# Loading Q and K in 1-KB runs and restoring the token order after the transpose

## The chip, the cores and the metric

One core of a Trainium2 chip. The time is device microseconds of one execution. Runs of one kernel in the same rounds differ by up to 2.4%; comparisons use runs taken on the same chip in the same rounds. The engines: PE (TensorE), PEld (its weight loads), DVE (VectorE), ACT (ScalarE), POOL (GpSimd), SP (SyncE, which issues most DMAs).

## The reference, cut to what matters

```python
# q, k, v: 8 batches x 8 heads x 576 tokens x 64; w_in 512x2048; w_out 2048x512
scores = scale * q @ k.T ; mask: key in (query-64, query] ; attn = softmax(scores)
x = attn @ v                      # 4608 tokens x 512
h = x @ w_in ; g = h * clip(h + 3, 0, 6) / 6 ; out = g @ w_out
```

## The kernel before: the parts that matter

The tokens go through the feed-forward part in nine blocks of 512. Block T has a first phase (x @ w_in, eight chunks of 8 matmuls; for each chunk ScalarE makes t, VectorE makes gT) and a second (gT @ w_out, 64 matmuls). The attention of batch T+1 is slipped in between the second phase's matmuls as side units: S (scores of one pair of heads), PV, and so on. A small planner fixes, before anything runs, the order of instructions on every engine; at run time each engine takes its own list in order: in the prediction's views VectorE stands 3.05 us at a cast whose data have not landed, with a gT behind it.

Batches 2 to 7 load Q and K with one token to a partition, and a DMA transpose turns them:

```python
def load_nat(b):                                 # before; cut
    for i, src in enumerate((q, k)):
        for kb in range(KB):                     # 128 tokens at a time, 256-B runs
            nc.sync.dma_start(out=st.rearrange("p (h d) -> p h d", h=H),
                in_=src[b, :, kb*P : kb*P+ss, :].rearrange("h s d -> s h d"))
            ...                                  # GpSimd casts st into natural[i]
        ...                                      # then, on SP:
        nc.sync.dma_start_transpose(out=QK_tiles[...], in_=natural[i])
```

The scores of one pair of heads: 18 matmuls with the keys as weights and 64 queries as moving side, then exp on ScalarE in two parts, from PSUM into pT, then the mask on VectorE:

```python
for part in range(2):                            # before; cut
    st = two_banks(...)                          # one of 3 PSUM slots, shared with the first phase
    for i in range(i0, i1):
        for h in range(2):
            nc.tensor.matmul(st[:, h, c:c+D], lhsT=kwin(b, g, i, h),
                             rhs=QT[h*D:(h+1)*D, i*D:(i+1)*D], start=True, stop=True)
    nc.scalar.activation(out=pT[:, :, i0*D:i1*D], in_=st[:, :, 0:(i1-i0)*D], func=EXP, scale=scale)
```

V of these batches is loaded by DMAs that ScalarE issues between its own instructions.

The softmax here doesn't subtract the row's maximum and nothing guards it: scores larger than these inputs give would overflow.

## Time and profile before

| | |
|---|---|
| time, median of the 3 runs known at first | 313.49 us (310.9 to 315.31) |
| the profiled run | 315.82 us, span 314.1, mean granted clock 0.989 |
| busy share | PE 95%, DVE 51%, ACT 50%, POOL 38% |
| DMA packets under 512 B | 142,064 of 153,487 |

### The profile page before, as it was taken

What the parts mean: (1) busy time and instruction counts of PE and PEld (TensorE: products, weight loads), DVE (VectorE), ACT (ScalarE), POOL (GpSimd) and SP (SyncE); (2) the same over time, 40 slices, a digit from 0 to 9 for tenths busy, and PEclk for the clock granted to TensorE, in tenths of its full rate; (3) what the DMA queues carried; (4) which work ended last, traced back from release to release, by engine and by line L of the source; (5) the groups of instructions that cost most, each with busy time, mean ns of one, the idle gap of its engine ahead of it and who ended that gap; (6) DMA issues with size and microseconds to landing.
All of it is one profiled execution on the core that took longest, in us unless ns stands there. A gap on an engine that the chain in (4) does not pass through costs nothing.

```text
span 314.1 us, 6662 instructions
## 1 busy us (share of the span) xinstructions
PE 297.4 (95%) x2746; PEld 154.8 (49%) x2787; DVE 161.5 (51%) x206; ACT 157.7 (50%) x200; POOL 118.6 (38%) x186
## 2 busy tenths in 40 slices
PE   7989699889899999999999999999999999999996
PEld 3554345544444444685444444444575444444443
DVE  5576553855761666166616671667066607404610
ACT  5946556445723672367236723672367326315611
POOL 2257466614862484256325742384243000000000
PEclk9999969999999999999999999999999999999999
DMA  8999999999999999999999999999990530020011
GB/s 230 252 369 389 388 272 240 241 194 199 204 193 205 214 212 177 192 272 201 205 155 267 208 174 197 246 204 173 206 239 21 116 106 0 18 84 34 0 66 69
DMA packets 153487, 58.38 MB, mean 186 GB/s; under 512 B 142064, under 2 KB 143344, under 8 KB 153456
## 3 DMA queue, kind: packets, MB, share of 16 engines
q1 hardware_dynamic: 125184, 50.80, 77.2%
q10 hardware_dynamic: 28272, 7.15, 12.5%
q8 instruction: 22, 0.36, 0.5%
q14 instruction: 9, 0.07, 0.1%
HBM read 36.70 MB, written 9.44 MB: 147 GB/s over the span
## 4 chain that ended last, share of the span: by engine, by line
PE 78%; DMA 11%; DVE 3%; SPq 3%; POOL 2%; issue 2%; ACT 0%; POOLq 0%; ACTq 0%
PE acc L815 37%; PE ps L767 32%; DMA st<-in_k_dram 5%; PE ps L672 3%; DMA st<-in_v_dram 3%; DMA st<-in_moe_w_in_dram 3%; PE ps L648 3%; SPq L329 2%; POOL runs L277 1%; SPq L412 1%; DVE pT L614 1%; PE ps L562 1%; DVE opg L713 1%; DVE pT L618 1%; DVE QKT L274 0%
## 5 line engine op out<-in xcount | busy, mean ns | idle before, releaser
L779 DVE SCALAR_TENSOR_TENSOR gT<-t,ps 128x1024 bf16<-128x1024 bf16 x72 | 87.6, 1220 | 101.3 <-ACT t L776 101.2
L815 PE MATMUL acc<-wout,gT 128*128 128x512 bf16 (+2 forms) x560 | 130.3, 377 | 3.2 <-issue 2.6
L767 PE MATMUL ps<-xT,win 128*128 128x512 bf16 (+4 forms) x695 | 125.6, 340 | 0.5
L776 ACT ACTIVATE t<-ps,half 128x1024 bf16<-128x1024 f32 x72 | 79.8, 1113 | 50.6 <-PE ps L767 49.6
L767 PEld LDWEIGHTS <-win 128*128 128x128 bf16 x704 | 65.2, 98 | 59.3
L815 PEld LDWEIGHTS <-gT 128*128 128x128 bf16 x592 | 54.2, 99 | 59.9 <-issue 2.6
L832 ACT COPY osb<-acc 128x512 f32<-128x512 f32 (+2 forms) x37 | 21.3, 575 | 77.6 <-PE acc L815 74.0
L277 POOL CAST runs<-st 64x512 bf16<-64x512 f32 x48 | 30.0, 624 | 72.7 <-DMA st<-in_v_dram 67.9
L277 POOL CAST nat<-st 128x512 bf16<-128x512 f32 x48 | 34.3, 726 | 17.3 <-DMA st<-in_k_dram 11.7
L654 ACT ACTIVATE pT<-ps 128x640 bf16<-128x640 f32 (+1 forms) x48 | 28.8, 650 | 10.5 <-PE ps L648 10.5
L713 DVE TENSOR_TENSOR opg<-ps,rec 128x640 bf16<-128x640 f32 x32 | 26.4, 824 | 1.1
L658 DVE TENSOR_TENSOR pT<-pT,mask 128x1152 bf16<-128x1152 bf16 x24 | 20.0, 832 | 6.2 <-ACT pT L654 6.2
L277 POOL CAST V<-st 128x512 bf16<-128x512 f32 (+1 forms) x30 | 18.1, 604 | 5.0 <-DMA st<-in_v_dram 3.5
L602 ACT ACTIVATE pT<-ps 128x768 bf16<-128x768 f32 x16 | 12.6, 820 | 2.1 <-PE ps L593 2.1
L648 PEld LDWEIGHTS <-QKT 64*128 64x128 bf16 x432 | 7.7, 95 | 11.1 <-issue 11.1
L672 PE MATMUL ps<-runs,pT 128*64 128x65 bf16 x288 | 12.4, 197 | 0.2 <-POOL runs L277 0.2
L672 PEld LDWEIGHTS <-pT 128*64 128x64 bf16 x480 | 9.6, 111 | 6.0 <-issue 3.3
L710 DVE RECIPROCAL rec<-ps 128x10 f32<-128x10 f32 x32 | 7.0, 217 | 10.1 <-PE ps L672 8.6
L648 PE MATMUL ps<-QKT 64*128 64x64 bf16 x432 | 10.6, 191 | 1.3 <-DVE gT L779 0.8
L277 POOL CAST wout<-st 128x1024 bf16<-128x1024 f32 x8 | 9.1, 1167 | 6.5 <-DMA st<-in_moe_w_out_dram 6.5
L672 PE MATMUL ps<-V,pT 128*64 128x65 bf16 x192 | 11.5, 198 | 0.0
L562 PE MATMUL ps<-ident,runs 64*64 64x64 bf16 x288 | 7.0, 199 | 4.1 <-DVE gT L779 2.7
(60 smaller groups left out, 122.0 us busy)
## 6 DMA issues: line engine op xcount, KB each, us to landing
out_dram<-osb SPq DMA_DIRECT2D x35, 256.0 KB, 3.7
st<-in_q_dram SPq DMA_DIRECT2D x24, 256.0 KB, 6.4
st<-in_k_dram SPq DMA_DIRECT2D x24, 256.0 KB, 5.6
st<-in_v_dram ACTq DMA_DIRECT2D x24, 256.0 KB, 6.1
st<-in_moe_w_out_dram SPq DMA_DIRECT2D x4, 1024.0 KB, 13.6
st<-in_moe_w_in_dram SPq DMA_DIRECT2D x3, 1024.0 KB, 10.4
st<-in_q_dram SPq DMA_DIRECT2D x8, 288.0 KB, 6.8
st<-in_k_dram SPq DMA_DIRECT2D x8, 288.0 KB, 6.9
```

The costliest lines, as they stand in the source:

```text
L277: return lambda s: nc.gpsimd.tensor_copy(out=out_ap, in_=in_ap) and None
L602: nc.scalar.activation(out=pT[:, :, kbs[0] : kbs[0] + 2, 0:QW], in_=st[:, :, 0 : 2 * QW].rearrange("p h (k w) -> p h k w", k=2), func=EXP, ...
L648: nc.tensor.matmul(st[:, h, c : c + D], lhsT=kwin(b, g, i, h), rhs=QT[h * D : (h + 1) * D, i * D : (i + 1) * D], start=True, stop=True,)
L654: nc.scalar.activation(out=pT[:, :, i0 * D : i1 * D], in_=st[:, :, 0 : (i1 - i0) * D], func=EXP, scale=scale,)
L658: pl.op("DVE", t, 0.8, lambda s: nc.vector.tensor_tensor(out=pT.rearrange("p h (i w) -> p (h i) w", w=D), in0=pT.rearrange("p h (i w) -> p ...
L672: nc.tensor.matmul(o[odd * D : (odd + 1) * D, h, m * VW : (m + 1) * VW], lhsT=pT[:, h, i * D : (i + 1) * D], rhs=(V if i % 2 else W)[:, g, ...
L713: nc.vector.tensor_tensor(out=opg[:].rearrange("p k h d -> p h k d"), in0=ov[:, :, :, 0:D], in1=rec[:].unsqueeze(3).to_broadcast([P, 2, KB ...
L767: nc.tensor.matmul(hT[:, j, dst : dst + w], lhsT=win16[:, g, (2 * c + j) * P : (2 * c + j + 1) * P], rhs=xT[:, g, src : src + w], start=(g ...
L776: nc.scalar.activation(out=t1[:], in_=hT[:], func=RELU, bias=half[:], scale=1.0 / 6.0)
L779: nc.vector.scalar_tensor_tensor(out=gT[:, 2 * c : 2 * c + 2, :], in0=cell["t"][:], scalar=1.0, in1=hT[:], op0=MIN, op1=MULT,)
L815: nc.tensor.matmul(accs[ts][:, c0:c1], lhsT=gT[:, fc, ts * P : (ts + 1) * P], rhs=wout16[:, fc, c0:c1], start=(fc == 0), stop=(fc == NFC - 1),
L832: nc.scalar.copy(out=osb[:, c0:c1], in_=acc[:, c0:c1])
```

## The change

Its intent: four successive tokens to a partition make runs of 1 KB in place of 256 B, a quarter of the packets. The transpose then delivers the tokens in the order (j p) in place of (p j). Keys must be in token order for the windows, so five copies straighten K^T. Queries stay turned through the matmul, and exp's write puts them right.

```diff
+            for hh in range(2):                  # load: 4 tokens to a partition, 4 heads at a time
+                nc.sync.dma_start(out=T["t"][:, 4*hh : 4*hh+4, :],
+                    in_=src[b, 4*hh : 4*hh+4, 0 : J*P, :].rearrange("h (p j) d -> p h (j d)", j=J))
...
+            def straighten(t):                   # after K's transpose; POOL or DVE, as the planner finds
+                copy_op("kn", KN_ENG, NG*D, t, KN[:, :, D+J*P : D+S], Kp[:, :, J*P : S], None, one)
+                for g in range(NG):
+                    copy_op("kn", KN_ENG, J*P, t, KN[:, g, D : D+J*P].rearrange("d (p j) -> d p j", j=J),
+                            Kp[:, g, 0 : J*P].rearrange("d (j p) -> d p j", j=J), None, one)
...
-   nc.tensor.matmul(st[:, h, c:c+D], ..., rhs=QT[h*D:(h+1)*D, i*D:(i+1)*D])
+   nc.tensor.matmul(st[:, h, ...].rearrange("k (j i p) -> k i j p", ...)[:, i-i0], ..., rhs=turned(i)[...])
...
-   out=pT[:, :, i0*D:i1*D], in_=st[:, :, 0:(i1-i0)*D]
+   out=pT[:, :, i0*D:i1*D].rearrange("k h (p j) -> k h j p", j=J),
+   in_=st[:, :, 0:(i1-i0)*D].rearrange("k h (j p) -> k h j p", j=J)
...
-VGAP2 = 1.3                                      # pace of batch 2's V loads
+VGAP2 = 2.2
-FIRST = [(0, f, g) ...]                          # places of batch 1's side units
+FIRST = ((6, "T", 0), (12, "T", 1), (16, "S", 0), (0, "T", 2), ...)
```

More of the change, by code (lines that the diff above doesn't have):

```diff
@@ L23 @@
 NPT = 4
+KN_ENG = ("POOL", "DVE")
 VGAP = 1.8
-VGAP2 = 1.3
+VGAP2 = 2.2
 VRATE = 150
@@ L122 @@
     KB = (S + P - 1) // P
+    J = S // P
     SP = KB * P
@@ L197 @@
     W_ring = [runs_flat[:, i * NV : (i + 1) * NV].rearrange("p (g k h w) -> p g k h w", g=NG, k=KB, h=2) for i in range(2)]
+    KN = runs_flat[:, 2 * NV : 2 * NV + NG * (D + S)].rearrange("p (g t) -> p g t", g=NG)
     BL = S // D
@@ L246 @@
     pl.op("DVE", 26.2, 0.1, lambda s: nc.vector.tensor_copy(out=mask64[:], in_=m64[:]) and None, "mask64", deps=("m64",))
+    pl.op("DVE", 0.0, 0.2, lambda s: nc.vector.memset(KN[:, :, 0:D], 0.0) and None, "knz", deps=(("T", NR6 - 1, NG - 1),))
     for i, t in enumerate(W_ring):
@@ L281 @@
         "spread": lambda e, n: {"DVE": 0.156, "ACT": 0.165}[e] + {"DVE": 1.04e-3, "ACT": 0.83e-3}[e] * n,
+        "kn": lambda e, n: {"DVE": 0.08, "POOL": 0.18}[e] + {"DVE": 1.04e-3, "POOL": 0.83e-3}[e] * n,
         "x": lambda e, n: {"DVE": 0.156, "ACT": 0.165}[e] + {"DVE": 0.52e-3, "ACT": 0.83e-3}[e] * n,
@@ L426, in load_nat @@
             n = natural[i]
-            deps = stage_slot([("cast", b, i, j) for j in range(KB - 1)])
+            deps = stage_slot([("cast", b, i, g) for g in range(NG)])
             if b > NR6:
@@ L444, in tr @@
                     d += (("s1", b - 1),)
-                pl.op("SP", t, 0.1, fn, ("tr", b, i), deps=d)
-            for kb in range(KB):
-                ss = min(P, S - kb * P)
-                def go(s, i=i, src=src, kb=kb, ss=ss, T=T, n=n, tr=tr):
-                    if kb == 0:
-                        T["t"] = stage.tile([P, 4, H * D], F32, name="st", tag="st")
-                    if kb == KB - 1:
-                        st = tails.tile([P, H * D], F32, name="tl", tag="tl")[:ss, :]
-                    else:
-                        st = T["t"][:, kb, :]
+                pl.op("SP", t, 0.1, fn, ("tr", b, i), straighten if i else None, deps=d)
@@ new lines, in straighten, with one @@
+            def straighten(t):
+                Kp = QK_tiles[b % NQT][:, NG : 2 * NG, :]
+                left = [NG + 1]
+                def one(t, g=None):
+                    left[0] -= 1
+                    if not left[0]:
+                        pl.mark(("kn", b), t)
+                copy_op("kn", KN_ENG, NG * D, t, KN[:, :, D + J * P : D + S], Kp[:, :, J * P : S], None, one)
+                for g in range(NG):
+                    copy_op("kn", KN_ENG, J * P, t, KN[:, g, D : D + J * P].rearrange("d (p j) -> d p j", j=J),
+                            Kp[:, g, 0 : J * P].rearrange("d (j p) -> d p j", j=J), None, one)
@@ L455, in go, with done @@
+            def done(t, T=T, tr=tr):
+                T["left"] -= 1
+                if not T["left"]:
+                    tr(t)
+            for hh in range(2):
+                def go(s, i=i, src=src, hh=hh, T=T, n=n, done=done):
+                    if hh == 0:
+                        T["t"] = stage.tile([P, H, J * D], F32, name="st", tag="st")
                     nc.sync.dma_start(
-                        out=st.rearrange("p (h d) -> p h d", h=H),
-                        in_=src[b, :, kb * P : kb * P + ss, :].rearrange("h s d -> s h d"),
-                    )
@@ L459, in go @@
-                    fr, land = moved(s, 262 * ss / P, 205)
-                    def done(t):
-                        T["left"] -= 1
-                        if not T["left"]:
-                            tr(t)
-                    pl.op("POOL", land, 0.61,
-                          cast_op("POOL", n[:ss, :, kb, :], st.rearrange("p (g d) -> p g d", g=NG)),
-                          ("cast", b, i, kb), done)
-                    return fr
-                yield b, deps + tail_slot([("cast", b, i, kb)]) if kb == KB - 1 else deps, go
+                        out=T["t"][:, 4 * hh : 4 * hh + 4, :],
@@ new lines, in go @@
+                        in_=src[b, 4 * hh : 4 * hh + 4, 0 : J * P, :].rearrange("h (p j) d -> p h (j d)", j=J),
+                    )
+                    fr, land = moved(s, 524, 330)
+                    for g in (2 * hh, 2 * hh + 1):
+                        pl.op("POOL", land, 0.62, cast_op(
+                            "POOL", n[:, g, 0:J, :].rearrange("p j (h d) -> p h j d", h=2),
+                            T["t"][:, 2 * g : 2 * g + 2, :].rearrange("p h (j d) -> p h j d", j=J)),
+                            ("cast", b, i, g), done)
@@ new lines, in go @@
+                    return fr
+                yield b, deps, go
+            def go(s, i=i, src=src, n=n, done=done):
+                st = tails.tile([P, H * D], F32, name="tl", tag="tl")[: S - J * P, :]
+                nc.sync.dma_start(
+                    out=st.rearrange("p (h d) -> p h d", h=H), in_=src[b, :, J * P : S, :].rearrange("h s d -> s h d"))
+                fr, land = moved(s, 131, 205)
+                pl.op("POOL", land, 0.61,
+                      cast_op("POOL", n[: S - J * P, :, J, :], st.rearrange("p (g d) -> p g d", g=NG)),
+                      ("cast", b, i, NG), done)
+                return fr
@@ L469, in load_nat @@
+            yield b, deps + tail_slot([("cast", b, i, NG)]), go
         stream_v(b)
@@ L534, in ready @@
         elif f[0] == "S":
-            ks = [("tr", b, g)] if b < NR6 else [("tr", b, i) for i in range(2)]
+            ks = [("tr", b, g)] if b < NR6 else [("tr", b, 0), ("kn", b)]
             if b == 0:
@@ L573, in scores @@
     def scores(b, g, which=(0, 1)):
-        for r in [("tr", b, g)] if b < NR6 else [("tr", b, i) for i in range(2)]:
+        for r in [("tr", b, g)] if b < NR6 else [("tr", b, 0), ("kn", b)]:
             pl.wait(r)
@@ L627, in kwin @@
     def kwin(b, g, i, h):
-        t = QK_tiles[b % NQT]
-        c = (2 * g + 1 if b < NR6 else NG + g) * SP + (i - 1) * D
-        return t[:].rearrange("p a s -> p (a s)")[h * D : (h + 1) * D, c : c + P]
+        return KN[h * D : (h + 1) * D, g, i * D : i * D + P]
     def blocks(b, g):
@@ L637, in scores64, with turned @@
     def scores64(b, g):
-        for i in range(2):
-            pl.wait(("tr", b, i))
+        pl.wait(("tr", b, 0))
+        pl.wait(("kn", b))
         QT, pT = qk(b, 0, g), blocks(b, g)
+        def turned(i):
+            if i == BL - 1:
+                return QT[:, i * D : (i + 1) * D].rearrange("d (p j) -> d j p", j=J)
+            return QT[:, 0 : J * P].rearrange("d (j p) -> d j p", j=J)[:, :, i * (D // J) : (i + 1) * (D // J)]
         for part in range(2):
@@ L646, in scores64 @@
                 for h in range(2):
-                    c = (i - i0) * D
                     nc.tensor.matmul(
-                        st[:, h, c : c + D], lhsT=kwin(b, g, i, h), rhs=QT[h * D : (h + 1) * D, i * D : (i + 1) * D],
+                        st[:, h, 0 : (i1 - i0) * D].rearrange("k (j i p) -> k i j p", j=J, i=i1 - i0)[:, i - i0],
+                        lhsT=kwin(b, g, i, h), rhs=turned(i)[h * D : (h + 1) * D],
                         start=True, stop=True,
@@ L654, in ex @@
                 nc.scalar.activation(
-                    out=pT[:, :, i0 * D : i1 * D], in_=st[:, :, 0 : (i1 - i0) * D], func=EXP, scale=scale,
+                    out=pT[:, :, i0 * D : i1 * D].rearrange("k h (p j) -> k h j p", j=J),
+                    in_=st[:, :, 0 : (i1 - i0) * D].rearrange("k h (j p) -> k h j p", j=J),
+                    func=EXP, scale=scale,
                 )
@@ L875 @@
     acc_pool = ctx.enter_context(tc.tile_pool(name="acc", bufs=2, space=PSUM))
-    FIRST = [(0, f, g) for f, g in (
-        ("T", 0), ("T", 1), ("S", 0), ("T", 2), ("S", 1), ("T", 3), ("S", 2), ("PV", 0), ("S", 3),
-        ("PV", 1), ("X", 0), ("PV", 2), ("X", 1), ("PV", 3), ("X", 2), ("X", 3))]
+    FIRST = ((6, "T", 0), (12, "T", 1), (16, "S", 0), (0, "T", 2), (0, "S", 1), (0, "T", 3),
+             (0, "S", 2), (0, "PV", 0), (0, "S", 3), (0, "PV", 1), (0, "X", 0), (0, "PV", 2),
+             (0, "X", 1), (0, "PV", 3), (0, "X", 2), (0, "X", 3))
     REST = ((4, "S", 0), (10, "S", 1), (17, "S", 2), (17, "PV", 0), (23, "S", 3), (23, "PV", 1),
```

## The prediction

> **What bounds the kernel now.** I read the views in this order: the page's busy lines and slices, the chain that ended last, a table of stretches, then the timelines of the places where TensorE stands still. The page:
>
> ```profile
> PE 297.4 (95%) x2746; PEld 154.8 (49%) x2787; DVE 161.5 (51%) x206; ACT 157.7 (50%) x200; POOL 118.6 (38%) x186
> ...
> PEclk9999969999999999999999999999999999999999
> ...
> DMA packets 153487, 58.38 MB, mean 186 GB/s; under 512 B 142064, under 2 KB 143344, under 8 KB 153456
> ...
> PE 78%; DMA 11%; DVE 3%; SPq 3%; POOL 2%; issue 2%; ACT 0%; POOLq 0%; ACTq 0%
> L779 DVE SCALAR_TENSOR_TENSOR gT<-t,ps 128x1024 bf16<-128x1024 bf16 x72 | 87.6, 1220 | 101.3 <-ACT t L776 101.2
> ```
>
> TensorE is busy 95% of the span and is 78% of the chain. Nearly all packets are under 512 B, which is what the change attacks, but the 11% of the chain that is DMA lies early. One slice of clock shows a 6. By stretch (length; busy time and count of PE, its loads, DVE, ACT, POOL; clock; DMA share; GB/s):
>
> ```profile
> 20.00:30.00 10.00, 9.33 (x51) 4.38 (x50) 6.15 (x9) 5.11 (x6) 5.76 (x6) 1.00 1.04 389
> 38.50:45.40 6.90, 5.88 (x55) 3.08 (x57) 3.81 (x4) 5.32 (x8) 4.32 (x4) 0.51 1.09 337
> 45.40:98.00 52.60, 48.82 (x518) 25.49 (x526) 29.81 (x38) 25.41 (x37) 27.97 (x43) 1.00 1.17 204
> 98.00:130.00 32.00, 31.43 (x282) 15.39 (x286) 16.74 (x20) 16.41 (x21) 15.46 (x23) 1.00 1.19 210
> 98.00:270.00 172.00, 169.38 (x1571) 89.72 (x1594) 93.03 (x107) 88.42 (x109) 67.67 (x105) 1.00 0.99 179
> ```
>
> From 98 to 270 us TensorE is idle 172.00 - 169.38 = 2.6 us in all, though the DMA engines are full for much of that time at half the rate that they reach early on. So the slow loads of batches 3 to 7 already lie hidden behind matmuls. What can be won is before 98 us: there TensorE stands still 3.8 us in the third row (52.60 - 48.82), about 2.7 us just before, and the second row runs at half clock. Those places:
>
> ```profile
> 37.21 0.76 PE L562 MATMUL ps<-ident,runs 64*64 64x64 bf16 x36 [1.65 <-DVE gT L779]
> ...
> 39.30 1.17 PE L562 MATMUL ps<-ident,runs 64*64 64x64 bf16 x36 [1.02 <-DVE gT L779]
> ...
> 80.80 0.29 PE L648 MATMUL ps<-QKT 64*128 64x64 bf16 x8 [0.81 <-DVE gT L779]
> ...
> 35.40 0.63 DVE L274 CAST runs<-st 128x576 bf16<-128x576 f32 x1 [3.05 <-DMA st<-in_q_dram]
> 35.95 1.21 DVE L779 SCALAR_TENSOR_TENSOR gT<-t,ps 128x1024 bf16<-128x1024 bf16 x1
> ```
>
> The last two lines matter most for what follows. VectorE takes its instructions in a fixed order. A cast whose data had not landed held it for 3.05 us, a gT product behind it came late, and TensorE, which needs the PSUM space that gT frees, stood still 1.65 us. That is a head-of-line wait, and the change places new ones.
>
> [...] 389 GB/s at a share of 1.04 with long packets, 210 at 1.19 with 256-B ones. Packet times read from the trace are 21 to 25 ns at 256 B and 46 to 52 at 1 KB, twice the bytes in a unit of time. [...] the new GpSimd copies read with a step of 256 B. [...] the half-clock stretch lasts 6.8 us and follows 3.4 us (35.1 to 38.5) in which TensorE did little.
>
> **The change part by part.**
>
> *The loads.* Q and K of a batch move 8192 packets of 256 B in their main loads, and 2048 of 1 KB after. On 16 engines that is 8192 x 21..25 / 16 = 10.8 to 12.8 us of DMA time before, 2048 x 46..52 / 16 = 5.9 to 6.7 after: about 5.5 us of every 32 us block. But the data were in time already (2.6 us idle in 172), so I put the direct gain from 98 us on at 0. The count of casts on GpSimd stays (five per tensor), about 0.73 us each.
>
> *The straightening.* After K's transpose lands, five copies put K back into token order: two of 128x512 on VectorE, two of 128x512 and the tail on GpSimd. VectorE per copy: its casts of 128x576 take 485 ns, so at least 0.45; a copy of 1152 elements from PSUM took 1358, so up to 0.6[...]. Two are 0.9 to 1.85 us. GpSimd: 2.5 x 0.73 = 1.8 us[...]. GpSimd is busy under half of 98 to 130, so it has room.
>
> The place in the order decides. In the instruction order of the changed program, the two VectorE copies of batches 3 to 7 stand after the fourth of the eight gT products of the block before, and four gT wait behind them. A block's first phase in before:
>
> ```profile
> 95.57 8.28 SPq L434 DMA_TRANSPOSE QKT<-nat  x2
> ...
> 97.77 13.98 PE L767 MATMUL ps<-xT,win 128*128 128x512 bf16 x63
> ...
> 106.03 1.22 DVE L779 SCALAR_TENSOR_TENSOR gT<-t,ps 128x1024 bf16<-128x1024 bf16 x1 [0.51 <-ACT t L776]
> 108.17 2.54 DVE L779 SCALAR_TENSOR_TENSOR gT<-t,ps 128x1024 bf16<-128x1024 bf16 x2 [0.92 <-ACT t L776]
> ...
> 112.55 0.44 PE L648 MATMUL ps<-QKT 64*128 64x64 bf16 x18
> ```
>
> The phase starts at s = 97.94 for batch 3. The fourth gT ends at 106.03 + 1.22, or s + 9.3. K's transpose is the second of the pair: issued at 99.89, landed 8.4 us later at 108.31. In this way K lands 10.4, 9.6, 10.3, 10.5 and 11.9 us after s for batches 3 to 7. So VectorE, done at s + 9.3, would stand 0.3 to 2.6 us at the copy, then work 0.9 to 1.85 us. The phase has eight chunks of 1.727 us (13.98 / 8 is near it) and three PSUM slots: the eighth chunk starts at s + 12.1 and needs the fifth gT done. With 1.22 us for gT and 0.1 for the handover, VectorE must be free by s + 10.8. Landing + copies - 10.8 gives stalls of 0.5 to 1.5, 0 to 0.8, 0.4 to 1.4, 0.6 to 1.6 and 2.0 to 3.0 us: 3.5 to 8.3 together. Against it: fewer packets should make the transposes land sooner, since issue to landing varies from 6.7 to 9.3 us among batches with the same work. If a third of the spread (0.9 us) is won in each batch the sum is 0.8 to 4.5 us. I count +3.5 us, in five stalls ahead of the eighth chunk.
>
> *The score matmuls.* Their right side is read in four runs of 16 columns and they write PSUM in four runs of 16. There are 432 of them, 24 units of 18 at 0.37 to 0.44 us, about 10 us in all. If runs cost nothing: 0. If 10% more: +1 us. I count +1. exp writes in steps of 8 B instead of contiguously; ACT is half idle, so 0.
>
> *The early part.* In the second phase of block 0 the first three side units of batch 1 move from accumulator counts 2, 4 and 5 to 6, 12 and 16. TensorE has then other work while it waits for the late gT, so the 1.65 may fall to about 0.9 and the 1.02 to 0; with fewer gaps the half clock may not come, which would save about 3 us (half of 6.8). But batch 1 still loads in the old way, its last Q and K land at 44 to 46 us, and the later units wait for them. Of 1.8 + 3 I count 2 us. For batch 2, K should land near 70 us in place of 75.4, so the 0.81 at 80.80 may vanish; but its copies stand after the second gT of block 1's first phase (s = 64.9), and the sixth chunk needs the third gT done: a limit of s + 7.3 = 72.2. Landing at 69 to 71 plus 0.9 to 1.85 is 70 to 73. I count -0.5.
>
> Sum: -2 - 0.5 + 3.5 + 1 = +2 us on 313.5.
>
> **The rivals.** First, the early part wins whole and the copies are hidden: the half clock goes, the transposes land 2 us sooner since the queues are emptier, stalls stay under 1 us. Then -4.5 or so: 308 to 311. For it speaks that the changed kernel's units were plainly re-placed by hand; against it, that the later units of batch 1 still have their old data. Second, the access patterns cost: each of the 24 score units takes 0.15 us longer (+3.6 us), [...] and the straightened K comes after 112.55, where the first unit wants it: 319 to 322. Against it, 3 to 4 us lie between landing and that unit. Third, the GpSimd copies, which stand amid the casts of V, hold at their own head until K lands, so V of the next batch is late and the PV units wait: 1 us or less a block, since GpSimd is idle about half the time. Fourth, everything is hidden but the new waits too, because K lands earlier than the fourth gT ends: 312 to 314.
>
> **The range and the chances.** The gains end at about 5 us, since TensorE hardly idles after 98 us; the losses add up block by block and so reach further. Predicted 315.5 us, 309.5 to 321 in 8 of 10. Faster by over 2% needs under 307.2, more than the whole early idle time and clock loss give together with no stall: 0.05. Slower by over 2% needs over 319.8, the long end of the stalls or the second rival: 0.16. Within 2%: 0.79.
>
> **What would show it.** The page's packets under 512 B should fall by about 6 x 8192 = 49,000, the DMA share in 98 to 270 with it, and PE busy there should not. In the timeline of VectorE each of blocks 2 to 6 should show, after the fourth gT, a wait ended by the transpose of QKT of 0.3 to 2 us, then two copies of 0.45 to 0.9 us; and TensorE a gap before its eighth chunk whose releaser is gT. If that gap is missing, and the copies begin at once, the step on landing times was wrong. If the score units keep their 0.37 to 0.44 us, runs of 16 are free. If the clock shows no half stretch near 40 us, the early part gave more than I count. The prediction is wrong altogether if TensorE's idle time after 98 us falls, or its matmuls change in length elsewhere.

## More of the kernel before

The prediction shows the lines and how to read them. One group that it does not show turned out to matter, exp (the groups of ScalarE by shape: line, engine, operation, output and input, count, busy us and mean ns):

```profile
L654 ACT ACTIVATE pT<-ps 128x640 bf16<-128x640 f32 x24 | 16.9, 705 | 10.4 <-PE ps L648 10.3
L654 ACT ACTIVATE pT<-ps 128x512 bf16<-128x512 f32 x24 | 14.3, 595 | 0.2 <-PE ps L648 0.2
```

## The result, and the profile after

Median 339.69 us (339.0 to 342.02, 4 runs) against 312.37 us of before (4 runs). The ratio of the fast runs is 1.0875, 95% interval 1.0772 to 1.0978: 8.75% slower. (A ratio is the mean time of one kernel's fast runs over that of the other's in the same rounds, so not quite the ratio of the medians.) Executions over 1.5% slower than the fastest of the same kernel are left out of the means. The page after:

```profile
PE 306.1 (90%) x2787; PEld 156.5 (46%) x2787; DVE 168.8 (50%) x220; ACT 191.4 (57%) x199; POOL 135.6 (40%) x204
...
PEclk9999999979999999999999999999999999999999
...
DMA packets 116239, 58.38 MB, mean 173 GB/s; under 512 B 92528, under 2 KB 106096, under 8 KB 116208
...
PE 37%; DMA 28%; ACT 17%; POOL 5%; DVE 4%; SPq 4%; issue 3%; ACTq 1%; POOLq 0%
```

The packets under 512 B fell as planned, by 49,536, and all packets by 37,248. The clock line has a 7 near 70 us, in block 1's first phase; E6 comes back to it. PE's share of the chain that ended last fell from 78% to 37%, and DMA and ScalarE stand in it now. The first line holds the hint that the prediction should have been about: ACT's busy time rose by 34 us, from 157.7 to 191.4. Its only changed computation is exp:

```profile
L682 ACT ACTIVATE pT<-ps 128x640 bf16<-128x640 f32 x24 | 39.9, 1663 | 0.0
L682 ACT ACTIVATE pT<-ps 128x512 bf16<-128x512 f32 x24 | 34.1, 1420 | 0.0
```

705 ns became 1663, 595 became 1420. Where does the time go? The phases, from the starts of the first w_in and the first w_out matmul of each block in TensorE's timeline (us; the last column is the best version, experiment 12):

| phase | before | after | E12 |
|---|---|---|---|
| block 0, second | 29.94 | 25.69 | 25.65 |
| block 1, first | 13.82 | 18.24 | 13.81 |
| block 1, second | 19.05 | 20.41 | 18.81 |
| blocks 2 to 6, first | 13.81 to 13.97 | 15.38 to 15.90 | 13.81 to 13.98 |
| blocks 2 to 6, second | 17.68 each | 20.38 to 20.42 | 17.78 to 17.79 |
| blocks 7 and 8, each phase, to its last matmul | 13.8 to 14.0 | 13.8 to 14.0 | 13.8 to 14.0 |

Summed over the blocks, the first phases lost 13.1 us (4.42 in block 1, 8.65 in blocks 2 to 6), the second phases from block 1 on lost 15.0 (1.36 + five times 2.7), and block 0 gained 4.3; with 0.2 us more at the start and 0.3 at the end, that is the 24.3 us between the spans of 314.1 and 338.4. The column of before is from a run in the slow state. The fast profile of E4, the same kernel with only the early units placed otherwise, has 13.81 and 19.45 us in block 1, 13.8 to 14.0 and 17.68 from block 2 on, so all but block 0's row holds, to 0.4 us, between fast runs too. Two of the losses have their own lines. In TensorE's timeline of block 2 (start, length, what ran; in brackets the idle time before it and its releaser):

```profile
113.70 1.89 PE L797 MATMUL ps<-xT,win 128*128 128x512 bf16 x8 [1.93 <-DVE gT L809]
...
120.98 0.32 PE L675 MATMUL ps<-QKT,runs 64*128 64x64 bf16 x8 [0.25 <-ACT pT L682]
122.13 0.19 PE L702 MATMUL ps<-runs,pT 128*64 128x65 bf16 x1 [0.83 <-ACT pT L682]
...
125.20 0.32 PE L675 MATMUL ps<-QKT,runs 64*128 64x64 bf16 x8 [0.82 <-ACT pT L682]
```

The first line is the predicted stall ahead of the eighth chunk. The other three were not predicted: score units wait for a PSUM slot that exp has not emptied, and a PV waits for exp's result. VectorE at the same time:

```profile
107.78 1.22 DVE L809 SCALAR_TENSOR_TENSOR gT<-t,ps 128x1024 bf16<-128x1024 bf16 x1 [0.50 <-ACT t L806]
111.20 1.32 DVE L279 COPY runs<-QKT 128x512 bf16<-128x512 bf16 x2 [2.20 <-DMA QKT<-nat]
112.44 3.47 DVE L809 SCALAR_TENSOR_TENSOR gT<-t,ps 128x1024 bf16<-128x1024 bf16 x3
```

This is the head-of-line wait: after the fourth gT VectorE stands 2.20 us until K's transpose lands, copies for 1.32, and three gT run late in a row. The chain of waits of that block (start, length, link) tells both stories in order, 9.2 us of K's transpose first and exp later:

```profile
101.96 9.21 DMA QKT<-nat
111.20 1.32 DVE runs L279 x2
112.52 1.14 DVE gT L809
113.70 1.90 PE ps L797 x8
115.62 1.11 ACT t L806
116.74 2.18 ACT pT L682 x2
```

### The profile page after: what moved, and what is told of

It reads as the page before. It is cut to its first block, busy times and chain, and to the rows that moved or that the text cites. A ratio compares the mean times of both kernels' runs of the same rounds, so it can differ in the third digit from the quotient of the medians.

```text
span 338.4 us, 6689 instructions
## 1 busy us (share of the span) xinstructions
PE 306.1 (90%) x2787; PEld 156.5 (46%) x2787; DVE 168.8 (50%) x220; ACT 191.4 (57%) x199; POOL 135.6 (40%) x204
## 3 DMA queue, kind: packets, MB, share of 16 engines
q10 hardware_dynamic: 28272, 7.15, 11.1%
## 4 chain that ended last, share of the span: by engine, by line
PE 37%; DMA 28%; ACT 17%; POOL 5%; DVE 4%; SPq 4%; issue 3%; ACTq 1%; POOLq 0%
PE acc L845 20%; PE ps L797 14%; ACT pT L682 14%; DMA QKT<-nat 13%; DMA st<-in_v_dram 8%; DMA st<-in_moe_w_out_dram 5%; DMA st<-in_k_dram 2%; PE ps L702 2%; ACT t L806 2%; DVE gT L809 2%; DVE runs L279 2%; SPq L335 1%; ACTq L387 1%; POOL V L282 1%; SPq L360 1%
## 5 line engine op out<-in xcount | busy, mean ns | idle before, releaser
L797 PE MATMUL ps<-xT,win 128*128 128x512 bf16 (+4 forms) x704 | 128.8, 344 | 10.4 <-DVE gT L809 10.4
L845 PE MATMUL acc<-wout,gT 128*128 128x512 bf16 (+2 forms) x592 | 134.3, 374 | 1.3 <-POOL wout L282 1.3
L682 ACT ACTIVATE pT<-ps 128x640 bf16<-128x640 f32 (+1 forms) x48 | 64.0, 1541 | 0.0
L688 DVE TENSOR_TENSOR pT<-pT,mask 128x1152 bf16<-128x1152 bf16 x24 | 21.8, 909 | 29.1 <-ACT pT L682 29.1
L282 POOL CAST nat<-st 128x512 bf16<-128x512 f32 x48 | 32.9, 722 | 3.4 <-DMA st<-in_k_dram 2.1
L282 POOL COPY runs<-QKT 128x512 bf16<-128x512 bf16 (+1 forms) x18 | 18.4, 1054 | 17.1 <-DMA QKT<-nat 17.1
L675 PE MATMUL ps<-QKT,runs 64*128 64x64 bf16 x432 | 13.3, 194 | 7.4 <-ACT pT L682 7.3
L675 PEld LDWEIGHTS <-runs 64*128 64x128 bf16 x432 | 9.5, 94 | 18.7 <-issue 17.4
L279 DVE COPY runs<-QKT 128x512 bf16<-128x512 bf16 x12 | 8.3, 739 | 9.4 <-DMA QKT<-nat 9.3
L279 DVE CAST runs<-st 128x576 bf16<-128x576 f32 x14 | 7.3, 526 | 11.0 <-DMA st<-in_q_dram 7.4
L702 PE MATMUL ps<-V,pT 128*64 128x65 bf16 x192 | 11.4, 199 | 0.0
## 6 DMA issues: line engine op xcount, KB each, us to landing
st<-in_moe_w_out_dram SPq DMA_DIRECT2D x4, 1024.0 KB, 13.1
```

The source lines that it names most:

```text
L279: return lambda s: nc.vector.tensor_copy(out=out_ap, in_=in_ap) and None
L282: return lambda s: nc.gpsimd.tensor_copy(out=out_ap, in_=in_ap) and None
L675: nc.tensor.matmul(st[:, h, 0 : (i1 - i0) * D].rearrange("k (j i p) -> k i j p", j=J, i=i1 - i0)[:, i - i0], lhsT=kwin(b, g, i, h), rhs=tu ...
L682: nc.scalar.activation(out=pT[:, :, i0 * D : i1 * D].rearrange("k h (p j) -> k h j p", j=J), in_=st[:, :, 0 : (i1 - i0) * D].rearrange("k ...
L688: pl.op("DVE", t, 0.8, lambda s: nc.vector.tensor_tensor(out=pT.rearrange("p h (i w) -> p (h i) w", w=D), in0=pT.rearrange("p h (i w) -> p ...
L702: nc.tensor.matmul(o[odd * D : (odd + 1) * D, h, m * VW : (m + 1) * VW], lhsT=pT[:, h, i * D : (i + 1) * D], rhs=(V if i % 2 else W)[:, g, ...
```

## The experiments

**Theory A**: two separate costs, exp's scattered write (the 15 us in the second phases) and VectorE's wait for K (most of the 13 us in the first). **Rival B**: the score matmuls with their runs of 16 slow exp or themselves. **Rival C**: one cause only, the late straightened K, which delays everything behind it. The checker compares with the reference; it passed also the runs whose order is wrong on purpose (E1, E7, E8), so here it does not see an order of queries within a batch. That E2 and the versions built on it are right is argued from the code: the same element goes to the same place as in the changed kernel, only the walk differs.

### E1: exp writes contiguously (wrong)

```diff
-   out=pT[:, :, i0*D:i1*D].rearrange("k h (p j) -> k h j p", j=J), in_=st[...].rearrange(...)
+   out=pT[:, :, i0*D:i1*D], in_=st[:, :, 0:(i1-i0)*D]
```

> The changed kernel with one thing undone: exp writes its result contiguously, in the order in which PSUM holds it (so P is in a turned order and the result is wrong on purpose). All matmuls, copies and waits stay. Theory A, two separate costs: the six second phases that hold scores of batches 2 to 7 lost 1.4 + 5 x 2.7 = 15 us only because exp went from 0.65 to 1.54 us; exp returns to 0.6 to 0.7 us, these phases to about 17.7 us, the time to 340 - 15 = 325 (322 to 328). The first phases keep their stalls of 1.4 to 1.9 us. Rival B, the score matmuls: the runs of 16 in PSUM make exp's reads slow or the matmuls late; then exp stays over 1.2 us and the time over 334. Rival C, one cause: the late straightened K delays all that follows; then exp gets short but the second phases stay near 20 us and the time over 334.

322.63 us, ratio 1.0286 to before. exp is back at 706 and 594 ns, the second phases at 17.78 us in place of 20.4, and the first phases keep most of theirs (15.5 to 15.8 in blocks 2 to 5, 14.8 in block 6). B and C fall as explanations of the second phases: the same matmuls in runs of 16 and the same late K are still there.

### E2: the steps on the reading side

```diff
+   out=pT[:, :, i0*D:i1*D].rearrange("k h (p j) -> k h p j", j=J),
+   in_=st[:, :, 0:(i1-i0)*D].rearrange("k h (j p) -> k h p j", j=J)
```

> The changed kernel with the reordering moved to the other side of exp: it reads PSUM in steps of 64 or 80 fp32 values (256 or 320 B) and writes pT contiguously; the result is right. If what costs is the scattered write into SBUF alone, exp takes 0.6 to 0.75 us and the time is that of the contiguous exp, about 325. If any order with steps costs ScalarE the same on either side, exp stays at 1.4 to 1.7 us and the time at 338 to 341. Half way: reads with steps cost part of it, 330 to 335.

324.18 us, ratio 1.0355, and exp by shape:

```profile
L682 ACT ACTIVATE pT<-ps 128x640 bf16<-128x640 f32 x24 | 16.9, 706 | 9.8 <-PE ps L675 9.8
L682 ACT ACTIVATE pT<-ps 128x512 bf16<-128x512 f32 x24 | 14.3, 594 | 0.0
```

Reading PSUM in steps of 256 or 320 B took 706 and 594 ns, as E1's exp without steps did; the same reordering written into SBUF in steps of 8 B took 1663 and 1420, 2.4 times. One call written otherwise, same result, 15.5 us.

### E3: VectorE's copies one gT later

```diff
 def straighten(t):
+    t += 1.7          # the planner then puts the two copies after the fifth gT
```

> The changed kernel with the two straightening copies on VectorE one gT product later in each block (after the fifth in place of the fourth; after the third in block 1), and nothing else moved on TensorE. Theory A: the eighth chunk needs the fifth gT, which no longer stands behind the copies, so the stalls of 1.9, 1.4, 1.4, 1.6, 1.5 us in blocks 2 to 6 go, block 1 keeps part of its 2.6; first phases return to 13.8 to 14.2 us and the time to 340 - 9 = 331 (328 to 334), the second phases staying at 20.4. Rival C, the late K itself is the limit and the stall only moves: then TensorE waits as long for the straightened K at the first score unit, and the time stays at 337 to 341.

332.95 us, ratio 1.0599; the profiled run was slow (clock 0.985), so its lengths count only where a fast profile confirms them. The first phases of blocks 2 to 6 are 13.82 to 13.98 us, all stalls gone (so they are in E5's fast profile); the second ones stay at 20.4, as in the fast profile of the changed kernel. In the block shown before, the copies now follow a gT without a wait:

```profile
114.03 1.22 DVE L809 SCALAR_TENSOR_TENSOR gT<-t,ps 128x1024 bf16<-128x1024 bf16 x1 [0.51 <-ACT t L806]
115.24 1.54 DVE L279 COPY runs<-QKT 128x512 bf16<-128x512 bf16 x2
```

So C falls here too: K landed 10.5 to 11.4 us into these phases, at most 0.9 us sooner than in the changed kernel and still too late for the old place, and moving its copies by one place freed the first phases. Block 1's, though, got longer in this run (22.25 us, 6.8 of them at half clock): there K came 14 us into the phase and the copies stand after the third gT.

### E4: the kernel before with only the new places of batch 1's units

```diff
-FIRST = [(0, f, g) for f, g in (...)]
+FIRST = ((6, "T", 0), (12, "T", 1), (16, "S", 0), (0, "T", 2), ...)
```

> The kernel before with only the new places of batch 1's side units (6, 12, 16). The changed kernel's second phase of block 0 took 25.7 us against 29.9. If these places alone did it (no half clock, fewer waits for gT), this gives 312.4 - 4 = 308.5 (307 to 310) with that phase at 25 to 27 us. If it came from the faster loads of Q and K instead, the phase stays at 29 to 30 us and the time at 311.5 to 314.

312.85 us, ratio 0.9993 (0.9902 to 1.0083): no change in time, although block 0's second phase took 25.72 us in this profile. The two facts agree if the 29.94 us of before's profile are that run's own: it is the one with a half-clock stretch and a mean clock of 0.989, while most other runs of before had 0.993 to 1.0 and took 310 to 314 us. E8, further down, settles it: it keeps the old places, and in its fast profile block 0's second phase took 24.81 us, with no half-clock stretch there. So the early "gain" was a difference between two single executions.

### E5: E2 and E3 together

> Both one-line changes together: exp reads with steps and writes contiguously, and VectorE's two copies stand one gT later. If the two costs are separate they add: 340 - 16 - 9 = 315 us, with second phases at 17.8, first phases of blocks 2 to 6 at 13.8 to 14.0, and only block 1's first phase still long (17 to 22 us, as in the last runs, since there the copies still stand ahead of five gT when K lands 10 to 14 us into it). If they overlap, so that mending one shows the other, the time stays over 320.

315.4 us, ratio 1.0121. The two costs add, as A says. What is left sits in block 1's first phase, 16.84 us.

### E6: K ahead of Q, all copies on GpSimd (on E2)

```diff
-for i, src in enumerate((q, k)):
+for i, src in ((1, k), (0, q)):
-KN_ENG = ("POOL", "DVE")
+KN_ENG = ("POOL",)
...              # cut: the dependency of the V loads follows the new order; straighten(t): t += 3.0
```

> The candidate: exp reads with steps; K is loaded and transposed ahead of Q; all five copies on GpSimd, none on VectorE. If the waits behind the transposes are all that is left, K now lands about 6 us into the first phase in place of 11, GpSimd's 5.6 us of copies end near 12 us, before the first score unit at 14.8, and VectorE's gT runs undisturbed: all first phases 13.8 to 14.0, block 1 too, second phases 17.8: the time is that of the kernel before plus 6 x 0.1 us, less up to 1.4 us in block 1's second phase: 311 to 313.5. If the faster loads were worth something in themselves, it comes under 309. If GpSimd's copies hold up the casts of V, the second phases show waits of PV for V and the time is over 316.

315.16 us, ratio 1.0088: a miss. All phases from block 2 on are clean (13.8 and 17.8), but block 1's first phase takes 17.94 us, with nothing of the copies left on VectorE. So the largest single stall of the changed kernel has another cause. ScalarE's timeline in the changed kernel, at the start of block 1, and TensorE's line that waited (ACTq: DMA issues on ScalarE's queue):

```profile
59.80 6.48 ACTq L387 DMA_DIRECT2D st<-in_v_dram  x2
66.38 1.11 ACT L806 ACTIVATE t<-ps,half 128x1024 bf16<-128x1024 f32 x1 [6.02 <-PE ps L797]
...
68.80 0.38 PE L797 MATMUL ps<-xT,win 128*128 128x512 bf16 x1 [2.59 <-DVE gT L809]
```

Two issues of batch 2's V loads stand ahead of block 1's first t, and they took 6.48 us to issue. The phase began at 60.87, and where nothing holds it the first t starts 1.9 us later (62.69 for 60.77 in E9), so t comes 3.6 us late, then gT, then TensorE finds no PSUM slot. The releaser printed for t is PE, but by that count PE was done for it at about 62.8; t started at 66.38, 0.1 us after the two issues ended (59.80 + 6.48). In the kernel before, t comes first and a V load after it.

A stretch of half clock follows the wait. In the changed kernel the granted clock is 0.50 from 69.4 to 72.8 us, right after TensorE's wait (68.4 to 71.8 in E6); w_in matmuls follow each other there every 427 ns, and every 216 ns afterwards. That is 3.4 us at half rate, so an estimate of 1.7 us lost. With the 2.6 us of the wait it makes up nearly all of the 4.4 us that this phase lost. Not every such wait is followed by one: in E5, after a wait of 2.4 us at the same place, the clock stayed at 1.00.

### E7: what in the scattered write costs (wrong)

```diff
+   out = (b odd)  pT[...].rearrange("k h (p t) -> k h t p", t=2)      # step of 4 B, 2 runs
+   out = (b even) pT.rearrange("k h (j q) -> k h j q", j=J)[..., part] # 4 runs, no step
```

> The changed kernel, wrong on purpose, to see what in the scattered write costs. Batches 3, 5, 7: two runs with a step of 2 values (4 B). Batches 2, 4, 6: four runs without a step, with gaps between. With a step of 4 (8 B) the two sizes of exp took 1663 and 1420 ns, contiguous 706 and 594. If any step costs, and only the step, the odd batches show near 1.6 and 1.4 us and the even ones 0.7 and 0.6. If the cost grows with the distance, the odd ones lie half way, 1.0 to 1.3. If the breaks between runs cost [...], the even ones show 0.9 to 1.0.

324.57 us in its one look, beside 312.41 of before. exp in a stretch with an even batch, then in one with an odd batch:

```profile
L682 ACT ACTIVATE pT<-ps 128x640 bf16<-128x640 f32 x4 | 2.8, 706 | 1.6 <-PE ps L675 1.6
L682 ACT ACTIVATE pT<-ps 128x512 bf16<-128x512 f32 x4 | 2.4, 594 | 0.0
```

```profile
L682 ACT ACTIVATE pT<-ps 128x640 bf16<-128x640 f32 x4 | 3.6, 899 | 1.0 <-PE ps L675 1.0
L682 ACT ACTIVATE pT<-ps 128x512 bf16<-128x512 f32 x4 | 2.9, 736 | 0.0
```

Breaks between runs cost nothing here: 706 and 594 ns, as in E1 without them. A step of 4 B costs far less than the 1.0 to 1.3 us expected. The cost grew with the distance between neighbours: at 4 B 0.3 ns more for each element of a partition (193 / 640), at 8 B 1.5 ns (958 / 640). Larger distances were not tried.

### E8: the kernel before with only the scattered write (wrong)

```diff
-   out=pT[:, :, i0*D:i1*D], in_=st[...]
+   out=pT[:, :, i0*D:i1*D].rearrange("k h (p j) -> k h j p", j=4), in_=st[...].rearrange(...)
```

> The kernel before with one part of the change alone: exp writes in steps of 8 B (wrong on purpose). If this alone costs what it cost in the changed kernel, exp goes from 0.65 to 1.54 us, the six second phases from 17.7 (19.0) to about 20.4, and the time to 312.5 + 15 = 327.5 (325 to 330). If it needs the rest of the change to hurt, the time stays under 320.

328.38 us, ratio 1.052. exp at 1658 and 1416 ns, second phases at 20.35 to 20.76 us from block 2 on. One part alone, put into the good kernel, costs 16 us. With E1 the case against the write is closed from both sides.

### E9 and E10: batch 2's V behind block 1's first gT

```diff
 deps = ... (("pv", b-2, NG-1), ("issued", b, ...))
+       + ((("g", b-1, 0),) if b == NR6 else ())
-VGAP2 = 2.2
+VGAP2 = 1.3
```

E9 is this on E6, E10 the same on E5.

> The candidate of the run before (K first, all copies on GpSimd, exp reads with steps) with one thing more: batch 2's five V loads, which ScalarE issues, wait for block 1's first gT and stand behind its second relu with one relu between each, as in the kernel before; there two of them stood ahead of the first relu and held ScalarE for 6.0 us (59.81 to 65.93). If that hold is the 4.1 us by which block 1's first phase was still too long (17.9 against 13.8), that phase returns to 13.8 to 14.2 and the time to 315.2 - 4 = 311 (309.5 to 312.5), at or under the kernel before. If the phase was long for another reason, it stays over 16 us and the time over 313.5. If V(2) now comes too late, block 1's second phase shows waits for V's casts and exceeds 19.

314.26 us, ratio 1.009: a miss in time, a hit in cause. Block 1's first phase is 13.81 us in place of 17.94, so the hold of ScalarE, with the half clock that followed it and is gone as well, was those 4.1 us. But the second phase grew to 20.27:

```profile
82.36 0.23 PE L702 MATMUL ps<-runs,pT 128*64 128x65 bf16 x3 [2.06 <-POOL runs L282]
```

The last of V landed at 81.6, behind loads of batch 3's K and Q that had been issued in between, and PV waited for its cast. Whoever pulled V forward had a reason.

> The kernel with exp mended and VectorE's copies one gT later, with the same move of batch 2's V loads, but K still after Q and two copies on VectorE. If in block 1 the wait of VectorE for K and the hold of ScalarE lie over each other, taking away the hold alone uncovers the other: K lands some 10 us into the phase, the copies end near 12, and the seventh chunk needs VectorE free by 9; first phase 16 to 17.5 in place of 16.8, time 314 to 316. If the hold was all, 13.8 to 14.2 and 311 to 313.

316.82 us, ratio 1.0152; block 1's first phase 18.94 us, longer still than the 16 to 17.5 expected. Without ScalarE's hold, VectorE's wait for K comes out (TensorE waits 3.29 us for gT, and a half-clock stretch of 3.4 us follows from 74.8 us, by the same estimate 1.7 us more): in the changed kernel two waits lay over each other in this phase, and taking away either alone would have shown little.

### E11 and E12: V from SyncE's queue, then GpSimd's order

```diff
-nc.scalar.dma_start(out=st..., in_=v[b, ...])            # E11, on E6
+(nc.sync if b == NR6 else nc.scalar).dma_start(out=st..., in_=v[b, ...])
...              # cut: the planner's entries for these five issues move to SyncE too
```

> The last candidate: as the run with K first and all copies on GpSimd, but batch 2's five V loads are issued from SyncE's queue, behind batch 2's transposes and ahead of batch 3's K and Q, so that ScalarE is held by none of them and V no longer shares the queues with batch 3. If V's place is all that is left in the early blocks, block 0's second phase, block 1's first and its second take 25.8, 13.8 and 17.8 to 18.5 us, together 57.4 to 58.1 against 59.0 in the kernel before with the new places; all later second phases are 0.1 us longer than before: 311.5 - 1 + 0.5 = 311 (309.5 to 312.5). If the loads cannot land sooner, whoever issues them, TensorE waits again for GpSimd's casts of V in block 1's second phase, which stays at 19.5 to 21, and the time at 313 to 316.

321.26 us, ratio 1.0299: a clear miss. V now landed at 75.6, six us sooner, and block 1's second phase took 28.68 us, 10.2 of them at half clock. GpSimd's timeline:

```profile
70.96 0.62 POOL L282 CAST runs<-st 64x512 bf16<-64x512 f32 x1 [8.52 <-DMA st<-in_v_dram]
...
73.00 4.45 POOL L282 COPY runs<-QKT 128x256 bf16<-128x256 bf16 x5
...
80.40 1.17 POOL L282 CAST nat<-st 128x512 bf16<-128x512 f32 x2
```

K had landed at 66.2, but its copies stood behind V's first cast; and casts of batch 3's K stood among those of V. The planner had put them where its own guess of landing times said. E12 changes that order alone:

```diff
-    t += 3.0
+    t += 1.0                                     # K's copies ahead of V's casts
+if b == NR6 + 1:
+    deps += (("cast", NR6, 2, KB - 2),)          # batch 3's loads planned behind V's casts
```

> The run before landed V of batch 2 six us sooner (75.6 in place of 81.6) and yet lost: in GpSimd's order V's first cast stood ahead of the K copies, and casts of batch 3's K stood between those of V, whose last ended at 88.2. Here only GpSimd's order differs: the five K copies first (K had landed at 66.2, GpSimd stood idle until 71.0), then all casts of V, then batch 3's. If order was the cause, the K copies end near 71, V's casts near 81, block 1's second phase falls from 28.7 to 18 to 19.5 us and the time from 321 to 310.5 to 312.5, level with the kernel before or up to 0.4% under it. If the loads themselves are too late, the phase stays over 20.5 us and the time over 313.

311.35 us (310.52 to 312.13, 6 runs) against 311.96 of before, ratio 0.9966, 95% interval 0.9937 to 0.9995. A hit:

```profile
66.61 4.45 POOL L282 COPY runs<-QKT 128x256 bf16<-128x256 bf16 x5 [4.24 <-DMA QKT<-nat]
```

Block 1's second phase is 18.81 us. This version keeps the 1-KB loads and comes out level with the kernel before, perhaps 0.3% under it. From 98 us on its second phases are 0.1 us longer than before's. That is the price of the score matmuls' runs of 16: from start to start, the 72 of a phase take 1.71 us in E1's trace and 1.605 in before's, and the other matmuls of the phase take the same. In the window from 98 to 270 us of its profile TensorE is busy 172.00 of 172.00 us at a DMA share of 0.82, where before had 0.99: the DMA engines are relieved, and no one was waiting for them.

## Why the prediction was wrong

It said 315.5, in 309.5 to 321, with 5 in 100 parts for over 2% faster and 16 for slower. The time was 339.7. By its own steps:

1. **"exp writes in steps of 8 B instead of contiguously; ACT is half idle, so 0."** This failed, and alone it breaks the range: exp took 2.4 times as long, the second phases 15.0 us longer, and 16 us when put alone into the kernel before. Two errors in one clause. The price of a write with steps was taken as nothing although no line showed it. And "half idle" is an average over the span: inside a second phase the exps come in bursts, each holding one of three PSUM slots and each with a PV behind it. In ScalarE's timeline of block 2 two parts took 1.19 us before; after, four ran in a row for 5.33. Without this step the time would still have been 324.2 (E2), 3 us over the range, by items 2 and 3.
2. **The stalls ahead of the eighth chunk, +3.5 us.** Mechanism right, place right, releaser right; the size was off. Blocks 2 to 6 lost 8.65 us. The first sum of 3.5 to 8.3 nearly held it; the deduction that fewer packets would let K land sooner was wrong. Counted from the first w_in matmul, K landed 11.1 to 11.7 us into the phase, where before it had been 9.7 to 12.1. With these landings and the measured 1.34 us of copies, the prediction's own formula gives 8.6 us, so the landing was the term that was off. (Its sums were loose too: its landings give 3.5 to 8.0, and with 0.9 us won in each batch 1.1 to 3.7, not 0.8 to 4.5.) Issue to landing in block 2 was 9.2 us, where before had 8.4, although the DMA share from 98 to 270 us fell from 0.99 to 0.81.
3. **Block 1, counted at -0.5 us.** It lost 4.4 us in its first phase. The limit was looked for on VectorE alone; the V issues that the new order puts ahead of ScalarE's first t were not weighed. E6 and E9 show them to be 4.1 us, some 1.7 of it, by the estimate there, in the half clock that followed the wait, E10 that VectorE's wait lay underneath. That half clock could follow a new wait was not weighed: the prediction had half clock only as something to win.
4. **The early part, counted at -2 us.** Places alone: 0 (E4). The half clock that they were to avoid belonged to the profiled run: E8, with the old places, has none there. In the 3.4 us ahead of it TensorE was busy for 1.53 us; that fewer gaps would keep the half clock away was an estimate from this one stretch.
5. **The score matmuls, +1 us.** About right: 0.1 us a phase, 0.6 over six phases.
6. **The loads, 0 from 98 us on.** Right, by E12. The 2.6 us of idle time that the prediction read there were in part not idle: before's page counts 2746 PE instructions, the changed kernel's 2787, for programs with as many matmuls; records are missing, and the phase lengths agree.

Of the rivals, the second (access patterns cost) had the right kind of cause, and the wrong instruction: it priced the matmuls, and exp's write not at all. The third (GpSimd's copies hold up the casts of V) is half there in the changed kernel: GpSimd stood 17.1 us, five times, at its copies until K landed, and no PV waited for its casts. In E11, where the order was otherwise, PVs waited for them 7.4 us.

## What to carry to other kernels

Price every changed access pattern on every engine before calling the engine idle, and when an order must be restored somewhere, try each side of the instruction: here exp with the steps in the read of PSUM took 706 ns, as without any, and with the steps in the write to SBUF 1663. A wait placed in a fixed order holds what stands behind it, so put it where the next engine has slack, one place later if need be (E3: the first phases of blocks 2 to 6 from 15.38 to 15.90 us down to 13.82 to 13.98); and look for a second wait beneath the first, and for half clock after the wait (3.4 us of it in the changed kernel's block 1). Compare phases, not two single executions: an accident of one profiled run can pass for a gain of 4 us.

## What was measured of access patterns and issues

- ScalarE's writes into SBUF, exp of 128x640 in bf16: 706 ns contiguous (E1), 899 in steps of 2 elements (E7), 1663 in steps of 4 (the changed kernel).
- Breaks between contiguous runs of such a write: 706 ns with four runs, no more than without (E7). Reads of PSUM in steps of 256 and 320 B: 706 and 594 ns, no more than without steps (E2).
- Matmuls that write PSUM in four runs of 16 fp32 and read the moving side in four runs of 16: 1.71 us for the 72 of a phase (E1) where before had 1.605, 0.1 us more, 1.5 ns each.
- GpSimd's copies with a 256-B step took 1066 ns (median, E12) where casts of as many elements in contiguous runs took 609 (median, changed kernel): 75% more, though the two operations differ in their types. A copy of the same type without steps took 395 ns (the shortest, E12) for half as many elements.
- Issues of plain loads from ScalarE's queue: two V loads took 6.48 us in the changed kernel, where four of the five in E9 took 0.4 us each. Why these two took so long, no run here shows.
